# Summing K·q over the head dimension: one more halving on VectorE for most of K, and one shared PSUM bank and read for its first half

## The chip, the cores and the metric

One core of one Trainium2 chip runs the kernel. The metric is the device time of one execution in microseconds (us). Each experiment was timed in rounds together with the kernel before on the same chip.

## The reference

```python
# q: [8, 32, 1, 128], k and v: [8, 32, 4096, 128], all bf16
scores = einsum('bhqd,bhkd->bhqk', q, k) * 128 ** -0.5
attn = softmax(scores, axis=-1)
return einsum('bhqk,bhkd->bhqd', attn, v)
```

There is one query per head, 256 heads, and 537 MB of K and V that are each used once.

## The kernel before

A tile is 8 heads of K (or V): 128 partitions (16 to a head) by 256 keys by 128 numbers, 64 KB in each partition, 8.39 MB in all. There are 32 K tiles and 32 V tiles. Three buffers hold them in rotation, in the order K(t+1), V(t), K(t+2), V(t+1) and so on. By this order V(t) takes over the buffer of K(t), and K(t+1) that of an older V.

```python
kv_pool = ctx.enter_context(tc.tile_pool(name="kv_pool", bufs=SLOTS))   # SLOTS = 3

def product(t, lo, hi):                 # VectorE, in place in the K tile
    part = kt[:, lo:hi, :]
    tensor_tensor(out=part, in0=part, in1=q, op=mult)
    tensor_tensor(out=part[:, :, 0:64], in0=part[:, :, 0:64], in1=part[:, :, 64:128], op=add)
    if width_of(t, lo // UC) < D // 2:  # second half of K, tiles 1 to 28
        tensor_tensor(out=part[:, :, 0:32], in0=part[:, :, 0:32], in1=part[:, :, 32:64], op=add)

def sum_over_d(t, u):                   # TensorE: identity matmuls add column groups in PSUM
    n = width_of(t, u) // DS            # DS = 8 columns of 64 keys fill a bank
    for s in range(n):
        matmul(ps, lhsT=ident, rhs=kt[:, u*UC:(u+1)*UC, s*DS:(s+1)*DS], start=(s == 0), stop=(s == n-1))

def scores_of(t, u):                    # VectorE: the last 8 columns, out of PSUM
    tensor_reduce(out=sc[:, u*UC:(u+1)*UC], in_=ps, op=add)

# ... one tile in the steady part (cuts; Q = 64 keys):
product(t, 0, 2*Q);   sum_over_d(t, 0); sum_over_d(t, 1)
product(t, 2*Q, 3*Q); sum_over_d(t, 2); scores_of(t, 0); scores_of(t, 1)
product(t, 3*Q, C);   sum_over_d(t, 3); scores_of(t, 2)
values_loop(t - 1)                      # TensorE, 64 matmuls over V(t-1)
load("k", t + 1)                        # waits for values_loop(t - 2), which ran in the turn of tile t - 1
load("v", t)                            # waits for sum_over_d(t, 3), the last reader of K(t)
scores_of(t, 3); weights_of(t)
```

## Time and profile before

| | kernel before |
|---|---|
| time, median of the runs beside the changed kernel | 1251.66 us |
| load queue, share of 16 engines' span | 99.5% |
| VectorE / TensorE busy | 1021.9 us (82%) / 786.8 us (63%) |
| K landing to K landing, mean of tiles 2 to 29 | 38.86 us |
| V issue after K's landing, mean | 32.16 us |

"Landing" of a K here is the start of the first product on it, which waits for that load. The prediction shows the page's lines and one steady tile and says how to read them. One line of the view of waits adds who waited, for what, total us, times, longest.

```profile
DVE kt L191 <- DMA kt<-in_k_dram: 139.9, 28, 6.3
```

VectorE waits for K 28 times, 5.0 us each: it is ahead of the loads by that much.

### The profile page before, as it was taken

The page shows a single profiled execution, that of the slowest core. Times are in us where ns is not written, and L with a number is a line of the kernel's source. Part 1 is how long each engine was busy: PE and PEld are TensorE (multiplying, and loading weights), DVE is VectorE, ACT ScalarE, POOL GpSimd, SP SyncE. Part 2 cuts the span into 40 slices and gives each one's busy share as a digit, 9 for nine tenths or more (in the row PEclk, how much of TensorE's full clock was granted, in tenths as well). Part 3 has the DMA queues.
Part 4 walks back from the last instruction along what each step waited for, and adds up shares of the span by engine and source line. Part 5 has one row for each costly group of instructions (what it writes and reads, how often), then busy time and mean ns, then how long its engine had stood idle before and what let it go on. Part 6 is the DMA issues. An engine that isn't in the chain of part 4 may idle for free. (4 is left out here: it accounts for less than half of the span.)

```text
span 1250.2 us, 10842 instructions
## 1 busy us (share of the span) xinstructions
PE 786.8 (63%) x3116; PEld 299.6 (24%) x3116; DVE 1021.9 (82%) x495; ACT 166.1 (13%) x433; POOL 4.5 (0%) x24
## 2 busy tenths in 40 slices
PE   3366567666576655766558665577655776556755
PEld 1122123222232222322223222222222222212222
DVE  7887987878977789777798777987779877798783
ACT  0111011111011110111101111011110111101111
POOL 1000000000000000000000000000000000000000
PEclk9987788777888778877788777887778878779867
DMA  9999999999999999999999999999999999999997
GB/s 405 436 436 435 434 436 432 436 430 428 426 437 436 429 435 434 434 435 436 436 434 432 424 437 437 432 430 428 436 437 434 430 433 434 430 435 421 427 446 329
DMA packets 11432, 537.33 MB, mean 430 GB/s; under 512 B 1808, under 2 KB 2064, under 8 KB 2320
## 3 DMA queue, kind: packets, MB, share of 16 engines
q1 hardware_dynamic: 11072, 536.94, 99.5%
q8 instruction: 15, 0.25, 0.1%
q10 hardware_dynamic: 336, 0.07, 0.0%
q14 instruction: 9, 0.07, 0.0%
HBM read 536.94 MB, written 0.07 MB: 430 GB/s over the span
## 5 line engine op out<-in xcount | busy, mean ns | idle before, releaser
L191 DVE TENSOR_TENSOR kt<-kt,qb 128x8192 bf16<-128x8192 bf16 (+1 forms) x99 | 560.9, 5665 | 146.6 <-DMA kt<-in_k_dram 139.9
L211 PE MATMUL ps<-kt,ident 128*128 128x512 bf16 x800 | 278.4, 511 | 389.9 <-DVE kt L199 299.7
L294 PE MATMUL av<-vt,w 128*32 x1740 | 425.5, 397 | 4.6
L194 DVE TENSOR_TENSOR kt<-kt 128x4096 bf16<-128x4096 bf16 (+1 forms) x99 | 288.8, 2917 | 3.4
L294 PEld LDWEIGHTS av<-vt,w 128*32 x1740 | 173.4, 100 | 262.4 <-issue 119.5
L211 PEld LDWEIGHTS <-ident 128*128 128x128 bf16 x800 | 95.7, 120 | 565.4 <-issue 527.9
L223 DVE TENSOR_REDUCE sc<-ps 128x64 f32<-128x512 f32 x128 | 85.3, 685 | 54.0 <-PE ps L211 54.0
L248 ACT ACTIVATE e<-sc,nmax 128x256 bf16<-128x256 f32 x32 | 16.3, 508 | 706.7 <-DVE nmax L242 706.7
L255 ACT ACTIVATE w<-e,mine 128x256 bf16<-128x256 bf16 x256 | 105.6, 495 | 1.1
L199 DVE TENSOR_TENSOR kt<-kt 128x2048 bf16<-128x2048 bf16 x56 | 68.6, 1225 | 1.9
L351 ACT ACTIVATE comb<-av 32x512 bf16<-32x512 f32 (+1 forms) x32 | 18.8, 586 | 329.0 <-PEq L284 321.4
L280 PE MATMUL av<-vt,w 128*32 128x512 bf16 x116 | 47.2, 499 | 14.6 <-issue 13.1
L371 PE MATMUL op<-comb,pick 32*16 32x128 bf16 (+1 forms) x128 | 12.1, 213 | 20.7 <-ACT comb L351 20.7
L280 PEld LDWEIGHTS av<-vt,w 128*32 128x32 bf16 x116 | 6.9, 100 | 55.2 <-issue 55.2
L177 PE MATMUL qp<-qg,heads 8*128 8x128 bf16 x32 | 7.0, 217 | 16.7 <-ACT qg L175 16.7
L371 PEld LDWEIGHTS <-pick 32*16 32x16 bf16 (+1 forms) x128 | 8.7, 83 | 27.7 <-issue 27.3
L322 PE MATMUL av<-vt,w 128*32 128x512 bf16 x188 | 13.7, 418 | 2.3 <-DMA vt<-in_v_dram 2.3
L235 DVE TENSOR_REDUCE pmax<-sc 128x1 f32<-128x256 f32 x32 | 13.4, 420 | 1.1
L175 ACT ACTIVATE qg<-qh 8x128 bf16<-8x128 f32 x32 | 8.5, 266 | 33.5 <-PE qh L171 33.5
L171 PE MATMUL qh<-q_all,ident 128*8 128x128 bf16 x32 | 7.2, 225 | 8.7 <-DMA q_all<-in_q_dram 8.3
L179 ACT ACTIVATE qb<-qp 128x128 bf16<-128x128 f32 x32 | 8.9, 278 | 9.7 <-PE qp L177 9.7
L237 DVE TENSOR_SCALAR spread<-same,pmax 128x32 f32<-128x32 f32 x32 | 7.7, 242 | 1.1
(31 smaller groups left out, 47.7 us busy)
## 6 DMA issues: line engine op xcount, KB each, us to landing
kt<-in_k_dram SPq DMA_DIRECT2D x4, 4096.0 KB, 24.3
kt<-in_k_dram SPq DMA_DIRECT2D x4, 2048.0 KB, 13.0
vt<-in_v_dram SPq DMA_DIRECT2D x1, 4096.0 KB, 33.9
vt<-in_v_dram SPq DMA_DIRECT2D x1, 2048.0 KB, 38.5
vt<-in_v_dram SPq DMA_DIRECT2D x1, 1024.0 KB, 40.5
vt<-in_v_dram SPq DMA_DIRECT2D x1, 512.0 KB, 41.3
vt<-in_v_dram SPq DMA_DIRECT2D x31, 25.8
kt<-in_k_dram SPq DMA_DIRECT2D x29, 28.3
```

Of the source, the lines that this page charges most:

```text
L191: nc.vector.tensor_tensor(out=part, in0=part, in1=qb[:].to_broadcast([P, hi - lo, D]), op=ALU.mult)
L194: nc.vector.tensor_tensor(out=part[:, :, 0 : D // 2], in0=part[:, :, 0 : D // 2], in1=part[:, :, D // 2 : D], op=ALU.add,)
L199: nc.vector.tensor_tensor(out=part[:, :, 0 : D // 4], in0=part[:, :, 0 : D // 4], in1=part[:, :, D // 4 : D // 2], op=ALU.add,)
L211: nc.tensor.matmul(ps[:], lhsT=ident[:], rhs=kt[:, u * UC : (u + 1) * UC, s * DS : (s + 1) * DS], start=(s == 0), stop=(s == n - 1),)
L223: made = nc.vector.tensor_reduce(out=scs[t][:, u * UC : (u + 1) * UC], in_=sums.pop((t, u))[:], axis=AX.X, op=ALU.add)
L248: nc.scalar.activation(out=e[:], in_=sc[:], func=ACT.Exp, bias=nmax[:, 0:1], scale=scale, accum_out=esums[t // R][:, t % R : t % R + 1],)
L255: nc.scalar.activation(out=w[:, :, g, :], in_=e_g, func=ACT.Copy, scale=mine[:, 0, g : g + 1])
L280: pe.matmul(av, lhsT=wf[:, i * nw : (i + 1) * nw], rhs=vf[:, i * nv : (i + 1) * nv], **how)
L294: pe.matmul(av, lhsT=wf[:, bass.ds(ow + i * nw, nw)], rhs=vf[:, bass.ds(ov + i * nv, nv)], start=False, stop=False,)
L322: nc.tensor.matmul(avs[t][j * AG : (j + 1) * AG, :], lhsT=w[:, i, :, :], rhs=vt[:, c0 : c0 + CB, :], start=(i < TG), stop=(j not in group[ ...
L351: nc.scalar.activation(out=comb[0:n, :, :], in_=av[0:n, :, :], func=ACT.Copy)
L371: nc.tensor.matmul(ops[n][:], lhsT=pick[0:e, m, r, :], rhs=comb[0:e, m, :], start=(r == 0 and m == 0), stop=(r == R - 1 and m == CB - 1 an ...
```

## The change

The change moves work from TensorE to VectorE: each further halving of the 128 columns is one more add in place, and leaves half as many columns for the identity matmuls. With 16 columns left, the whole first half (128 keys by 4 columns) fits one bank, so four matmuls and one read do for it. Tile 0 and the last three keep their widths. The diff, cut:

```diff
-        return D // 4 if u >= NU // 2 and 0 < t < NT - 3 else D // 2
+        return (D // 4 if lo == C // 2 else D // 8) if 0 < t < NT - 3 else D // 2
 ... in product
+        n = D
+        while n > width_of(t, lo):
+            n //= 2
             nc.vector.tensor_tensor(
+                out=part[:, :, 0:n], in0=part[:, :, 0:n], in1=part[:, :, n : 2 * n], op=ALU.add
             )
 ... in sum_over_d
-        n = width_of(t, u) // DS
+        ds = BANK // (hi - lo)
+        n = width_of(t, lo) // ds
 ... in the tile loop (cut)
-                sum_over_d(t, 0)
+                sum_over_d(t, 0, HALF)
-                scores_of(t, 0)
-            scores_of(t, 1)
+                scores_of(t, 0, HALF)
```

More of the change, by code (lines that the diff above doesn't have):

```diff
@@ L43 @@
     scale = float(D) ** -0.5
-    UC = 64
-    DS = 512 // UC
-    NU = C // UC
+    BANK = 512
     CB = 4
@@ L180, in q_prep, with width_of @@
         qbs[t] = qb
-    def width_of(t, u):
-        return D // 4 if u >= NU // 2 and 0 < t < NT - 3 else D // 2
+    def width_of(t, lo):
+        return (D // 4 if lo == C // 2 else D // 8) if 0 < t < NT - 3 else D // 2
     def product(t, lo, hi):
@@ L193, in product, with sum_over_d, scores_of @@
         )
-        nc.vector.tensor_tensor(
-            out=part[:, :, 0 : D // 2], in0=part[:, :, 0 : D // 2],
-            in1=part[:, :, D // 2 : D], op=ALU.add,
-        )
-        if width_of(t, lo // UC) < D // 2:
+        n = D
+        while n > width_of(t, lo):
+            n //= 2
             nc.vector.tensor_tensor(
-                out=part[:, :, 0 : D // 4], in0=part[:, :, 0 : D // 4],
-                in1=part[:, :, D // 4 : D // 2], op=ALU.add,
+                out=part[:, :, 0:n], in0=part[:, :, 0:n], in1=part[:, :, n : 2 * n], op=ALU.add
             )
     sums = {}
-    def sum_over_d(t, u):
+    def sum_over_d(t, lo, hi):
         kt = loads["k", t]
-        ps = ps_s.tile([P, UC, DS], F32, name="ps", tag="ps")
-        n = width_of(t, u) // DS
+        ps = ps_s.tile([P, BANK], F32, name="ps", tag="ps")
+        ds = BANK // (hi - lo)
+        n = width_of(t, lo) // ds
         for s in range(n):
             nc.tensor.matmul(
-                ps[:], lhsT=ident[:],
-                rhs=kt[:, u * UC : (u + 1) * UC, s * DS : (s + 1) * DS],
+                ps[:], lhsT=ident[:], rhs=kt[:, lo:hi, s * ds : (s + 1) * ds],
                 start=(s == 0), stop=(s == n - 1),
             )
-        sums[t, u] = ps
+        sums[t, lo] = ps
     scs = {}
-    def scores_of(t, u):
-        if u == 0:
+    def scores_of(t, lo, hi):
+        if lo == 0:
             scs[t] = sc_pool.tile([P, C], F32, name="sc", tag="sc")
+        ps = sums.pop((t, lo))[:].rearrange("p (c s) -> p c s", c=hi - lo)
         made = nc.vector.tensor_reduce(
-            out=scs[t][:, u * UC : (u + 1) * UC], in_=sums.pop((t, u))[:], axis=AX.X, op=ALU.add
+            out=scs[t][:, lo:hi], in_=ps, axis=AX.X, op=ALU.add
         )
-        if u == NU - 1:
+        if hi == C:
             behind_loop(made)
@@ L392, in store_of @@
             nc.scalar.dma_start(o_n[s, :, lo : u + 1, :], stages[s][:, lo : u + 1, :])
-    Q = C // 4
+    Q, HALF = C // 4, C // 2
     load("k", 0)
@@ L408 @@
                 load("v", t)
-            product(t, 0, 2 * Q if loop else Q)
-            if not loop:
-                sum_over_d(t, 0)
+            if loop:
+                product(t, 0, HALF)
+            else:
+                product(t, 0, Q)
+                sum_over_d(t, 0, Q)
             if 0 < t - 1 <= LT:
@@ L419 @@
             if loop:
-                sum_over_d(t, 0)
+                sum_over_d(t, 0, HALF)
             else:
-                product(t, Q, 2 * Q)
-            sum_over_d(t, 1)
-            if not loop:
-                scores_of(t, 0)
-            product(t, 2 * Q, 3 * Q)
-            sum_over_d(t, 2)
+                product(t, Q, HALF)
+                sum_over_d(t, Q, HALF)
+                scores_of(t, 0, Q)
+            product(t, HALF, HALF + Q)
+            sum_over_d(t, HALF, HALF + Q)
             if loop:
-                scores_of(t, 0)
-            scores_of(t, 1)
+                scores_of(t, 0, HALF)
+            else:
+                scores_of(t, Q, HALF)
             if t > 2 and t % R == 1:
                 recip_of(n)
-            product(t, 3 * Q, C)
-            sum_over_d(t, 3)
-            scores_of(t, 2)
+            product(t, HALF + Q, C)
+            sum_over_d(t, HALF + Q, C)
+            scores_of(t, HALF, HALF + Q)
             if loop:
@@ L441 @@
                 values_of(t - 1, 0, C)
-            scores_of(t, 3)
+            scores_of(t, HALF + Q, C)
             weights_of(t)
```

## The prediction

> **What bounds the kernel now.** I read the page from the top: busy shares, the forty slices, the DMA queues, then the DMA issues.
>
> ```profile
> PE 786.8 (63%) x3116; PEld 299.6 (24%) x3116; DVE 1021.9 (82%) x495; ACT 166.1 (13%) x433; POOL 4.5 (0%) x24
> ...
> DMA  9999999999999999999999999999999999999997
> GB/s 405 436 436 435 434 436 432 436 430 428 426 437 436 429 435 434 434 435 436 436 434 432 424 437 437 432 430 428 436 437 434 430 433 434 430 435 421 427 446 329
> ...
> q1 hardware_dynamic: 11072, 536.94, 99.5%
> ...
> HBM read 536.94 MB, written 0.07 MB: 430 GB/s over the span
> ...
> vt<-in_v_dram SPq DMA_DIRECT2D x31, 25.8
> kt<-in_k_dram SPq DMA_DIRECT2D x29, 28.3
> ```
>
> Every slice but the last has the DMA engines at 90% or more, and the load queue fills 99.5% of 16 engines' span. VectorE is the busiest engine and has 18% of the span to spare. K and V have to be read once: 2 x 8 x 32 x 4096 x 128 x 2 bytes = 536.9 MB, which is what was read. The end is therefore set by the loads. The 64 KB packets of the trace take 2.42 us each, so 16 engines move 16 x 65536 / 2.42 = 433 GB/s, and 536.9 MB at that rate are 1239 us. The other 11 us of the 1250.2 us span are the launch before the first byte, the short packets at both ends and the work after the last V rows. The change touches none of these: the first tile and the last three keep two-fold halving and 64-column sums exactly as they are.
>
> The question is then only whether the changed compute still lets every load be issued before the queue runs dry. Three buffers hold K and V tiles of 8.39 MB. V of tile t goes into the buffer of K of tile t, so its issue waits for the last identity matmul that reads that K tile; the next K goes into the buffer of an older V, so its issue waits for the loop of value matmuls. I follow one steady iteration in the timeline (columns: start us, us, engine, line, operation, tiles, count, idle time before).
>
> ```profile
> 618.41 0.33 SPq L158 DMA_DIRECT2D vt<-in_v_dram  x1
> ...
> 619.63 14.81 PE L294 MATMUL av<-vt,w 128*32 x60
> ...
> 624.96 8.69 DVE L191 TENSOR_TENSOR kt<-kt,qb 128x16384 bf16<-128x16384 bf16 x1 [4.88 <-DMA kt<-in_k_dram]
> ...
> 633.69 4.42 DVE L194 TENSOR_TENSOR kt<-kt 128x8192 bf16<-128x8192 bf16 x1
> ...
> 635.26 0.33 SPq L158 DMA_DIRECT2D kt<-in_k_dram  x1
> ...
> 642.49 2.29 DVE L194 TENSOR_TENSOR kt<-kt 128x4096 bf16<-128x4096 bf16 x1
> 644.81 1.23 DVE L199 TENSOR_TENSOR kt<-kt 128x2048 bf16<-128x2048 bf16 x1
> 645.96 1.28 DVE L223 TENSOR_REDUCE sc<-ps 128x64 f32<-128x512 f32 x2
> ...
> 655.21 1.87 PE L211 MATMUL ps<-kt,ident 128*128 128x512 bf16 x4 [7.80 <-DVE kt L199]
> ...
> 657.11 0.33 SPq L158 DMA_DIRECT2D vt<-in_v_dram  x1
> ...
> 663.67 8.69 DVE L191 TENSOR_TENSOR kt<-kt,qb 128x16384 bf16<-128x16384 bf16 x1 [4.89 <-DMA kt<-in_k_dram]
> ```
>
> From K landing to K landing are 663.67 - 624.96 = 38.71 us, two tiles at 433 GB/s. VectorE has finished its tile and sits idle 4.9 us until the next K lands. V is issued 32.15 us after the K landing, 6.5 us before the queue needs it. The same lead comes out of the issue table: a V takes 25.8 us from issue to landing, of which a tile's transfer is 19.35 (half of 38.71), so it stood 6.4 us in the queue; a K stood 28.3 - 19.35 = 9.0 us. These two leads are the slack that the change spends.
>
> **What the Trainium skill says.** "VectorE: DVE Perf Modes", section "The perf-mode tier table": a bf16 tensor_tensor in SBUF reaches the 2x mode, 1224 ns for 2048 elements; a tensor_reduce has only 1x. The trace agrees: 1225 ns for the 128x2048 add, and 685 ns for a reduce of 512 fp32. "TensorE: Matmul & The Clock Gate", Part 1: after about 3.4 us of idling the array runs at half clock, 426.7 ns between matmuls of 512 columns against 215.7 warm. The trace agrees: the four matmuls ahead of each V issue, after 7.8 us of idling, take 1.87 us, whereas sixteen in a row at 638.17 take 3.61. "SBUF — State Buffer", section "Who interferes with whom": DMA and compute engines use separate SBUF ports, so a busier VectorE should not slow the loads. This trace neither contradicts nor isolates it: slices with VectorE at 7 and at 9 tenths both show 436 GB/s. "DMA: Bandwidth & Descriptors", Specifications, puts the fabric ceiling at 435 GB/s; the 433 of the packets is already there.
>
> **The change part by part**, for each of the 28 tiles 1 to 28.
> - Added on VectorE, first half: an add of 128x4096 (2.29 us) and one of 128x2048 (1.22). From start to start, which includes the handoffs, such adds cost 4.46, 2.32 and 1.15 (651.61 to 653.93 to 655.08 in the timeline for the last two). The half takes 8.73 + 4.46 + 2.32 + 1.15 = 16.66 us against 638.03 - 624.96 = 13.07: +3.59.
> - Removed: one of the two PSUM reads after the third quarter. Two took 1.19 start to next start, so one takes 0.60: -0.59. The new read still streams 512 elements and only writes 128 sums, so I keep 685 ns.
> - Added, last quarter: an add of 128x1024. The rows of 8192, 4096 and 2048 elements (4425, 2292, 1225 ns) lie on a line of 0.521 ns an element plus 158, giving 692 ns; with a handoff +0.73. The 8192 and 4096 rows differ in the number of runs, and the 2048 row has shorter runs, yet one line fits all three, so I charge nothing for runs of 16 elements.
> - Removed on TensorE: the first half needs 16 columns / 4 = 4 matmuls instead of 2 x 8, the last quarter 2 instead of 4: 14 fewer per tile, 392 in all, so 408 stay of 800. On the path to the V issue lie only the last quarter's: 1.87 us becomes about 1.87 - 2 x 0.427 = 1.02: -0.85.
>
> Sum on the path from K landing to V issue: 3.59 - 0.59 + 0.73 - 0.85 = **+2.9 us**. V's lead falls from 6.5 to about 3.6 us. The value loop starts right after those sums, as before, and starts cold as before, so I keep 16.85 us from V issue to K issue; K's lead falls from 9.0 to about 6.1 us. VectorE's idle time before each K tile falls from 4.9 to about 2.0 us. Busy time: VectorE + 28 x (2.29 + 1.22 + 0.69 - 0.69) = +98 us, to about 1120 us (90%). TensorE loses 392 matmuls; at 0.427 to 0.511 each (cold spacing and recorded mean) this is 170 to 200 us of 787, none of which the end waits for.
>
> None of the leads goes to zero, so no load starts later and **the sum at the end is 0**: predicted 1251.5 us, the time before. The tightest place is the start, where V of tile 1 is issued at 74.82 while K of tile 2 lands at 80.95. Its lead of about 6 us loses the same 2.9, so it is not lost either.
>
> **The rivals.** (a) VectorE becomes the bound. For it: at 90% the share looks near the limit, and the work per tile goes to about 36.7 us from first product to last statistic (33.8 now, 624.96 to 658.78, plus 2.9). Against: the loads give it 38.71. It would need another 2 us a tile; if adds over runs of 16 elements fell to the 1x rate, an estimate from 0.521 doubled is 2048 x 0.521 + 1024 x 0.521 = 1.6 us. That only just fits; if everything exceeded the period by 1 us, the kernel would be 28 us slower, about 1280. (b) The issue comes too late although VectorE has room: the lead of 3.6 us could be shorter than what a load needs between its issue and its first bytes. First evidence: the first K is issued at 0.81 us and bytes flow from about 1.9, so 1.1 us is enough. If each V left a bubble of 0.3 us, 28 x 0.3 = 8 us, 1260. (c) TensorE, with less work, stays cold longer and the value loop lengthens: entirely cold, 60 matmuls are 25.6 us instead of 14.8, K's lead of 6.1 would become -4.7, and 28 x 4.7 = 130 us would be added, 1380. Against it: the loop already begins cold after 8 us of idling in the profile and gets its full clock within 4 us, and the change leaves the loop itself alone. (d) A gain: fewer matmuls and more granted clock. All of it lands in idle time of TensorE; even with no DMA idling at all the 0.5% that the queue leaves free are 6 us, 1245.
>
> **Range and chances.** The three runs of before lie within 0.3 us, and I expect the loads to set the same pace, so the range is narrow: 1249.8 to 1255.0. The upper side allows a few small bubbles of (b) or a slow add of (a). A gain over 2% (25 us) would need the loads to run above the rate they hold now: 1%. A loss over 2% needs (a) or (c) in full: 3%. Within 2%: 96%.
>
> **What would show it.** Right: DMA slices as before; VectorE near 1120 us; 100 PSUM reads; 408 sum matmuls; idle time before the products on K landing falling from 139.9 to about 60 us; V from issue to landing near 22.9 us and K near 25.4; the chain of waits still ending in the V loads. Wrong: adds of 128x2048 with runs of 16 well above 1.22 us, V landing 20 us or less after its issue, DMA slices at 8 tenths, products no longer waiting for K loads, or a value loop over 20 us. A period above 38.8 us between K landings would make the prediction wrong.

## The result, and the profile after

The changed kernel takes **1267.32 us** (1265.66 to 1268.20, four runs) against 1251.66 us: ratio 1.0123, interval 1.0108 to 1.0138. It is within 2%, as forecast, but 15.7 us slower and far outside the predicted range of 1249.8 to 1255.0.

The page of the changed kernel (busy shares, DMA slices, load queue, rate over the span, chain that ended last, issue to landing):

```profile
PE 688.0 (54%) x2724; PEld 252.0 (20%) x2724; DVE 1122.4 (89%) x550; ACT 166.0 (13%) x433; POOL 4.4 (0%) x24
...
DMA  9999999999999999999999999999999999999998
...
q1 hardware_dynamic: 11072, 536.94, 99.2%
...
HBM read 536.94 MB, written 0.07 MB: 424 GB/s over the span
...
DMA vt<-in_v_dram 3%; DVE kt L189 1%; PE ps L207 0%; PE av L318 0%; DVE kt L195 0%; SPq L156 0%; DVE sc L219 0%; PE op L359 0%; ACT stage L378 0%; PE op L367 0%; DVEq L219 0%
...
vt<-in_v_dram SPq DMA_DIRECT2D x31, 24.2
kt<-in_k_dram SPq DMA_DIRECT2D x29, 26.7
```

The DMA slices look exactly as full as before, yet the same bytes come at 424 GB/s, not 430. A share of 99% does not say that the engines move bytes at their full rate: it counts the time that packets are under way. One steady tile of the timeline shows the compute side:

```profile
634.05 8.69 DVE L189 TENSOR_TENSOR kt<-kt,qb 128x16384 bf16<-128x16384 bf16 x1 [2.17 <-DMA kt<-in_k_dram]
...
642.77 8.01 DVE L195 TENSOR_TENSOR kt<-kt 128x8192 bf16<-128x8192 bf16 x3
...
647.21 0.33 SPq L156 DMA_DIRECT2D kt<-in_k_dram  x1
...
658.62 0.69 DVE L219 TENSOR_REDUCE sc<-ps 128x128 f32<-128x512 f32 x1
...
663.67 4.28 DVE L195 TENSOR_TENSOR kt<-kt 128x4096 bf16<-128x4096 bf16 x3
...
668.01 1.03 PE L207 MATMUL ps<-kt,ident 128*128 128x512 bf16 x2 [7.36 <-DVE kt L195]
...
669.07 0.33 SPq L156 DMA_DIRECT2D vt<-in_v_dram  x1
...
673.43 8.69 DVE L189 TENSOR_TENSOR kt<-kt,qb 128x16384 bf16<-128x16384 bf16 x1 [2.68 <-DMA kt<-in_k_dram]
```

The adds, the read and the two last matmuls cost what was worked out, and V is issued 669.07 - 634.05 = 35.02 us after K's landing. By form, the adds have these means (28 of the 84 work on runs of 16 elements, the others on 32; all 28 of the second line on 16):

```profile
L195 DVE TENSOR_TENSOR kt<-kt 128x2048 bf16<-128x2048 bf16 x84 | 102.9, 1225 | 2.9
L195 DVE TENSOR_TENSOR kt<-kt 128x1024 bf16<-128x1024 bf16 x28 | 19.4, 691 | 1.0
```

VectorE is still not the bound: it waits for K in every tile. In the view of waits:

```profile
DVE kt L189 <- DMA kt<-in_k_dram: 74.6, 28, 4.1
```

That is 2.7 us a tile, more than the 2.0 predicted, because the landings themselves now come later: 39.38 us apart here, 39.43 in the mean. Over the 27 intervals from tile 2 to tile 29, 39.43 - 38.86 makes 15.6 us: the whole loss.

So the loads are slower although the queue never shows as empty. The trace also has each 64 KB packet with start and duration (7680 of them). I joined packets to engines by their times (the record does not name the engine, so such chains can swap where two engines' times coincide). Start and duration, both in us, of a few engines around the V issue at 669.07 in the changed kernel:

```
663.55:2.42 665.96:2.42 668.38:2.43 670.80:3.15 673.95:2.42 676.37:2.42
663.48:2.42 665.90:2.44 668.33:2.45 670.78:3.14 673.92:2.42 676.33:2.42
664.54:2.43 666.96:2.42 669.38:2.42 671.80:2.68 674.48:2.42 676.90:2.42
662.86:2.42 665.27:2.42 667.69:2.50 670.18:2.70 672.89:2.42 675.30:2.42
```

In each engine shown, the packet that starts 1 to 3 us after the issue takes 2.7 to 3.2 us, where nearly all others take 2.42 (the longest of the run near an issue takes 4.1). In the last row this packet still belongs to K: the stretch does not spare the engines that are behind. In the changed kernel 534 packets last over 2.5 us, before only 52. Most of them start from 1 to 5 us after a V issue; there is no such crowd after K issues. Summed over the packets from one V issue to the following K issue and divided by 16 engines, the time over 2.42 us plus the time in which engines carried no packet is 0.65 us a tile against 0.03 before; 27 tiles of the difference are 16.7 us. That is about the loss again, from the other side.

**Theory A** follows: V is issued too late. Not later than the landing of K, but later than the moment at which the engines have taken their last K packet and want the first of V. A tile is 128 packets, so in order of start the first packet of V can be counted off. It starts 2.9 us before "K has landed" in the kernel before. Little of that is the wait from the last packet's end to the product: the last K packet of the tile shown ends at 672.97, 0.46 us ahead of 673.43. The rest is that the 16 engines are not in step. The trace has sixteen finish signals for each load, each some 0.3 us after a packet's end; those of this K come from 671.04 to 673.31, so the first engine needs V's packets while the last still carries K. In the kernel before, the signals of one K lie 1.7 us apart at tile 3 and 4.2 us apart at tile 26. So V's lead in the kernel before was not 6.5 us but 3.7 in the mean, and it falls along the run from 5.9 to 2.3 as the engines drift apart. In the changed kernel it is 1.6 in the mean, and never below 0.96: an engine then waits for the issue. (Reckoned from the first of K's finish signals, less 0.3 us, the two means are 3.7 and 1.5.) The **rival B** is that more VectorE work in SBUF slows the transfers themselves.

### The profile page after: what moved, and what is told of

Its sections match the earlier page's. It is cut to its first block, busy times and chain, and to the rows that moved or that the text cites. A ratio compares the mean times of both kernels' runs of the same rounds, so it can differ in the third digit from the quotient of the medians.

```text
span 1265.7 us, 10145 instructions
## 1 busy us (share of the span) xinstructions
PE 688.0 (54%) x2724; PEld 252.0 (20%) x2724; DVE 1122.4 (89%) x550; ACT 166.0 (13%) x433; POOL 4.4 (0%) x24
## 5 line engine op out<-in xcount | busy, mean ns | idle before, releaser
L195 DVE TENSOR_TENSOR kt<-kt 128x8192 bf16<-128x8192 bf16 (+2 forms) x239 | 475.2, 1988 | 8.2
L207 PE MATMUL ps<-kt,ident 128*128 128x512 bf16 x408 | 174.9, 578 | 508.5 <-DVE kt L195 508.2
L290 PE MATMUL av<-vt,w 128*32 x1740 | 429.9, 408 | 1.2
L290 PEld LDWEIGHTS av<-vt,w 128*32 x1740 | 178.9, 103 | 258.2 <-issue 101.2
L207 PEld LDWEIGHTS <-ident 128*128 128x128 bf16 x408 | 41.6, 122 | 634.8 <-DVE kt L195 571.1
L219 DVE TENSOR_REDUCE sc<-ps 128x64 f32<-128x512 f32 (+1 forms) x99 | 68.0, 687 | 31.0 <-PE ps L207 31.0
L175 PE MATMUL qp<-qg,heads 8*128 8x128 bf16 x32 | 7.0, 217 | 16.7 <-ACT qg L173 16.7
```

Of the source, the lines that this page charges most:

```text
L195: nc.vector.tensor_tensor(out=part[:, :, 0:n], in0=part[:, :, 0:n], in1=part[:, :, n : 2 * n], op=ALU.add)
L207: nc.tensor.matmul(ps[:], lhsT=ident[:], rhs=kt[:, lo:hi, s * ds : (s + 1) * ds], start=(s == 0), stop=(s == n - 1),)
L219: made = nc.vector.tensor_reduce(out=scs[t][:, lo:hi], in_=ps, axis=AX.X, op=ALU.add)
L290: pe.matmul(av, lhsT=wf[:, bass.ds(ow + i * nw, nw)], rhs=vf[:, bass.ds(ov + i * nv, nv)], start=False, stop=False,)
```

## The experiments

In each, "V at" is the mean delay from K's landing to V's issue, and "slow" counts the 64 KB packets over 2.5 us.

**1. The kernel before, V issued later, VectorE untouched.** Matmuls whose result is thrown away come ahead of the last sum:

```diff
+        for s in range(LATE if u == NU - 1 and 0 < t < NT - 3 else 0):   # LATE = 7
+            nc.tensor.matmul(ps[:], lhsT=ident[:], rhs=kt[:, u*UC:(u+1)*UC, 0:DS], start=True, stop=True)
         for s in range(n):
```

> The kernel before, with seven more identity matmuls (results thrown away) ahead of the last sum of each tile 1 to 28. VectorE's work is untouched; only the issue of V moves from 32.15 us after the landing of K to about 35, as in the changed kernel. Theory A (the V load is issued too late: its first packets run slow because its lead was shorter than I worked out): 1262 to 1272 us, and several hundred 64 KB packets over 2.5 us as in the changed kernel (534), not 52. Rival B (more VectorE work in SBUF slows the transfers themselves): 1251.5 us within 1, packets as before.

Measured: 1266.22 us against 1251.92 (ratio 1.0113, interval 1.0096 to 1.0130), V at 34.86 us, 444 slow packets. VectorE stays at its old load:

```profile
PE 822.6 (65%) x3312; PEld 308.1 (24%) x3312; DVE 1021.9 (81%) x495; ACT 166.1 (13%) x433; POOL 4.4 (0%) x24
```

The loss comes back without any of the change's VectorE work. A is right in kind and in size. K's issue moves with V's here, as in the changed kernel, because the value loop starts after the last sums. But counted in the same way, K's lead in the changed kernel is still 5.1 us in the mean (6.7 before) and never below 3.95, and only 4 of its 534 slow packets start 1 to 5 us after a K issue. So the late issue that costs is V's.

**2. The kernel before, VectorE busier, V issued as before.** Fifteen small adds on zeros after the statistics:

```diff
             weights_of(t)
+            if loop:
+                for _ in range(15):
+                    nc.vector.tensor_tensor(out=w_last[:, 0:LAST//2, :], in0=w_last[:, 0:LAST//2, :],
+                                            in1=w_last[:, LAST//2:LAST, :], op=ALU.add)
```

> The kernel before, with fifteen small adds on zeros (about 3.4 us a tile) on VectorE after the statistics of each tile 1 to 28, when it waits for the next K. VectorE busy rises to about 1115 to 1120 us as in the changed kernel; V is issued as before. Theory A (late issue): 1251.5 us within 1. Rival B (VectorE work slows the transfers): about 1267 us.

Measured: 1255.72 us, ratio 1.0029 (1.0013 to 1.0046), VectorE 1116.5 us, V at 32.17, 124 slow packets. Neither theory expected this: far from B's 1267, but 3.8 us over the time beside it, where A expected none. Experiments 5 and 6 look into it.

**3. The changed kernel, V issued 0.6 us earlier.** The read of the first half moves behind the last quarter's product:

```diff
-            if loop:
-                scores_of(t, 0, HALF)
-            else:
+            if not loop:
                 scores_of(t, Q, HALF)
 ...
             sum_over_d(t, HALF + Q, C)
+            if loop:
+                scores_of(t, 0, HALF)
             scores_of(t, HALF, HALF + Q)
```

> The changed kernel, with the PSUM read of the first half moved from before the last quarter's product to after it. The work is the same in sum, but the last sums and with them the issue of V come 0.6 us earlier (34.4 us after the landing of K, not 35.0). Theory A: most of the loss depends steeply on the lead, so part of it goes: 1256 to 1264 us. Rival B: 1267 us within 1.5.

Measured: 1259.02 us (ratio 1.0061, 1.0044 to 1.0078), V at 34.45, 228 slow packets. The same work in another order, 0.6 us earlier, saves over half of the loss: A.

**4. The changed kernel with half buffers.** Six buffers of half a tile, and two loads of 4 MB for each tile, so the first half of V waits only for the first half of K:

```diff
-    kv_pool = ...tile_pool(name="kv_pool", bufs=SLOTS)
+    kv_pool = ...tile_pool(name="kv_pool", bufs=2 * SLOTS)
-        buf = kv_pool.tile([P, C, D], ...)
-        for n in cuts.get((kind, t), [C]):
+        for n in cuts.get((kind, t), [H, H]):          # H = C // 2
+            h, x = divmod(c0, H)
+            if x == 0: buf[h] = kv_pool.tile([P, H, D], ...)
 ... (the value loop is cut in two, one for each half of V)
```

> The changed kernel, with each K and V tile in two half buffers and two loads of 4 MB: the first half of V needs only the first half of K to be done, so it is issued more than 15 us earlier. VectorE's work is the same 1122 us. Theory A: the loss is gone, 1249.5 to 1252.5 us, few packets over 2.5 us. Rival B: 1265 us or more.

Measured: 1257.41 us (ratio 1.0044, 1.0028 to 1.0061). The first half of V is issued at 18.39 us. Both expectations miss: 9.9 us of the loss are gone, 5.5 us stay. The packets are now 32 KB, and only 24 of 16000 last over 1.26 us, so none crowd after an issue. But they take 1.2176 us in the mean, where half a 64 KB packet of the kernel before takes 1.2119. That is 16000 x 0.0057 / 16 = 5.7 us. Experiment 12 is the control.

**5. The extra VectorE work as one instruction.**

```diff
             weights_of(t)
+            if loop:
+                spare = small.tile([P, 1], F32, name="spare", tag="spare")
+                nc.vector.tensor_reduce(out=spare[:],
+                    in_=loads["v", t - 1][:, 0:26, :].rearrange("p c d -> p (c d)"), axis=AX.X, op=ALU.add)
```

> The kernel before, with the extra VectorE work as one long reduce of 3328 elements of the V tile (about 3.6 us) in the idle time after the statistics, in place of the fifteen small adds that cost 3.8 us in the run before. Theory A (the fifteen adds cost through their number: more instruction fetches on the DMA engines, which push engines apart and eat the lead of V): 1251.9 us within 1. Rival B (VectorE traffic in SBUF while K lands and V starts slows the transfers): 1255 us or more.

Measured: 1252.81 us (ratio 1.0009, 0.9993 to 1.0026), 29 slow packets. VectorE is as busy as in experiment 2, and the time is that of before within the interval. So VectorE's busy time as such costs nothing that shows, and something else in experiment 2 does, the number of instructions being the likeliest. Of B this run tests little: it reads 3328 elements a tile, where the change adds three adds of 4096, 2048 and 1024 with two inputs and an output each. Against B stand experiments 1, 4 and 12.

**6. The fifteen adds, V issued 0.6 us earlier.** The kernel of experiment 2, with `scores_of(t, 1)` moved behind `sum_over_d(t, 3)`.

> The kernel with the fifteen small adds, and one PSUM read moved behind the last quarter's product, so V is issued 0.6 us earlier (31.55 us after the landing of K). VectorE's work is unchanged. Theory A: the earlier issue gives back most of the 3.8 us, 1251.5 to 1253.5 us. Rival B: 1255.5 us within 1.

Measured: 1255.50 us (ratio 1.0033, 1.0016 to 1.0049), V at 31.56, 78 slow packets. **A's expectation fails here**: slow packets go from 124 to 78 and the time does not move. The rows of instruction fetches in the DMA view (queue, packets, MB, share), first before, then the fifteen adds:

```profile
q8 instruction: 15, 0.25, 0.1%
q10 hardware_dynamic: 336, 0.07, 0.0%
q14 instruction: 9, 0.07, 0.0%
```

```profile
q8 instruction: 15, 0.25, 0.1%
q10 hardware_dynamic: 336, 0.07, 0.0%
q14 instruction: 13, 0.11, 0.0%
```

The 8 KB fetches of the last row run on the engines that carry the loads. One takes 0.31 us, and in several cases the load packet behind it takes up to 0.7 us more: that engine is then 1.0 us late. If it is the last engine to finish, the whole tile is. In the run with fifteen adds the landings are 38.7 us apart, but 39.63 to 39.67 at four tiles spaced four apart, each with such a fetch inside; in the kernel before only two intervals have this length (39.66 and 39.64). Not every fetch lengthens its tile. From tile 1 to tile 29 the landings take 2.9 us more in all than before, and moving the issue cannot help against an engine that is late by itself. Part of it is a short lead all the same: with the engines further out of step, V's lead is 3.05 us in the mean, though V's delay is unchanged, and 64 slow packets start 1 to 5 us after a V issue against 15 before. Experiment 6 brings the lead to 3.42 and these packets to 53 only. This rests on the traces and on experiment 5; I made no run that changes the fetches alone, so what the fifteen adds cost is argued and not shown.

**7. Four extra matmuls** in place of seven (`LATE = 4`).

> The kernel before with four extra matmuls ahead of the last sum, so that V is issued some 1.7 us later (about 33.8 us after the landing of K, between the kernel before and the changed one). Theory A: 1254 to 1260 us. Rival B: 1251.9 us within 1.

Measured: 1254.40 us (ratio 1.0018, 1.0001 to 1.0035), V at 33.80, 178 slow packets.

**8. Twelve extra matmuls** (`LATE = 12`).

> The kernel before with twelve extra matmuls, so that V is issued 36 to 37 us after the landing of K, later than in the changed kernel (35.05). Theory A: with no lead left the period is the issue's delay plus a fixed 4.4 us (39.43 - 35.05 in the changed kernel), 40.4 to 41.4 us, and the time 1290 to 1320 us. Rival B: 1251.9 us within 1.

Measured: 1273.78 us (ratio 1.0170, 1.0151 to 1.0190), V at 35.96, 559 slow packets. The loss grows, but less than I expected: the interval between landings is 39.74 us, 3.8 us over V's delay and not 4.4. The engines' lead differs from tile to tile, and the intervals scatter from 38.7 to 41.6, so a mean delay plus a constant is too crude.

**9. The first half's part of the change alone**: the last quarter is halved twice as before.

```diff
-        return (D // 4 if lo == C // 2 else D // 8) if 0 < t < NT - 3 else D // 2
+        return (D // 4 if lo >= C // 2 else D // 8) if 0 < t < NT - 3 else D // 2
```

> The part of the change in the first half alone: halved three times, one bank, one read; the last quarter is halved twice as before. By the sums of the prediction V is issued at 32.15 + 3.59 - 0.59 = 35.15 us after the landing of K, as in the changed kernel (35.05), though VectorE works 19 us less. Theory A: 1265 to 1269 us, as the changed kernel. A theory that goes by VectorE's share would give back about a fifth of the loss, 1264.

Measured: 1270.07 us (ratio 1.0145, 1.0128 to 1.0162), V at 35.18, 497 slow packets, and VectorE does 19 us less than in the changed kernel:

```profile
PE 711.9 (56%) x2780; PEld 254.2 (20%) x2780; DVE 1103.0 (87%) x522; ACT 166.1 (13%) x433; POOL 4.4 (0%) x24
```

Less VectorE work, and 1 us above A's range instead of below: the first half's adds carry the whole loss, and the last quarter's third halving gives a little back, as its sum of +0.73 - 0.85 says.

**10. The last quarter's part alone**, on the kernel before.

```diff
-        return D // 4 if u >= NU // 2 and 0 < t < NT - 3 else D // 2
+        return (D // 8 if u == NU - 1 else D // 4) if u >= NU // 2 and 0 < t < NT - 3 else D // 2
 ... (product adds the third halving where the width is D // 8)
```

> The part in the last quarter alone, on the kernel before: its third halving costs VectorE 0.73 us a tile and saves two cold matmuls, 0.85 us, ahead of the issue of V, so V is issued at about 32.0 us. Theory A: 1251.5 us within 1. By VectorE's share: 1254.

Measured: 1252.47 us (ratio 1.0007, 0.9990 to 1.0024), V at 32.04, 30 slow packets: no difference that this run can tell from none.

**11. The kernel before, V issued 0.6 us earlier** (`scores_of(t, 1)` moved as in experiment 6).

> The kernel before with one PSUM read moved behind the last quarter's product: V is issued 0.6 us earlier, at 31.55 us. Theory A: its loads hardly wait any more for V's issue, so little is to be had, 1250.8 to 1251.6 us.

Measured: 1251.57 us (ratio 1.0002, 0.9985 to 1.0019), V at 31.57, 22 slow packets. More lead than the kernel before has is worth nothing, so no order of this work will beat it by much.

**12. The kernel before with half buffers**, edited as in experiment 4.

> The kernel before with half buffers and 4 MB loads, the control for the changed kernel with half buffers (1257.4 us). If the 5.5 us left there come from the rows of 32 KB in place of 64 KB (16000 packets of 1.2176 us against half as many of 2.4218 are 6.6 us more on 16 engines), this kernel takes 1257 us too, within 1. If they come from VectorE's work, it takes 1251.6.

Measured: 1257.08 us (ratio 1.0044, 1.0027 to 1.0061). It is as slow as the changed kernel with half buffers, 1257.41. With V's issue out of the way, the two kernels are 0.3 us apart (their medians are from different rounds), though the changed one's VectorE is busy 1122.2 us and this one's 1021.9. The 5.5 us belong to the half buffers, and the longer packets account for them: with the mean of all 7680 packets, 2.4239 us (the expectation says 2.4218), its sum is 5.7 us.

Put in order of V's issue, kernels with quite different VectorE loads form one row:

| kernel | VectorE busy, us | V at, us | slow packets | time, us |
|---|---|---|---|---|
| before, read later (11) | 1021.9 | 31.57 | 22 | 1251.57 |
| last quarter alone (10) | 1041.2 | 32.04 | 30 | 1252.47 |
| before | 1021.9 | 32.16 | 52 | 1251.66 |
| four extra matmuls (7) | 1021.9 | 33.80 | 178 | 1254.40 |
| changed, read later (3) | 1120.4 | 34.45 | 228 | 1259.02 |
| seven extra matmuls (1) | 1021.9 | 34.86 | 444 | 1266.22 |
| changed | 1122.4 | 35.05 | 534 | 1267.32 |
| first half alone (9) | 1103.0 | 35.18 | 497 | 1270.07 |
| twelve extra matmuls (8) | 1021.8 | 35.96 | 559 | 1273.78 |

The knee lies between 32.16 and 33.80 us. No kernel tried beats the kernel before.

The traces allow a sharper sorting: by V's lead at every single issue, over these nine kernels and those of experiments 2, 5 and 6 (V of tiles 2 to 27, 312 issues). Packet time over 2.42 us from 2 us before V's issue to K's issue, and engine time without a packet from V's issue to K's, divided by 16 engines, make the loss at an issue:

| V's lead, us | mean loss, us: six kernels with VectorE at 1041 us or less | six kernels with VectorE at 1103 us or more |
|---|---|---|
| under 1 | 1.17 (25 issues) | 1.18 (12) |
| 1 to 2 | 0.43 (18) | 0.56 (48) |
| 2 to 3 | 0.14 (49) | 0.16 (50) |
| over 3 | 0.02 (64) | 0.02 (46) |

The loss goes with the lead, and a busy VectorE changes it little if at all: the largest difference, 0.13 us, is within the scatter of those issues.

## Why the prediction was wrong

- **The bound was read correctly.** The loads set the end before and after, and the chain of waits still ends in them.
- **The sums of the change were right.** V's issue was to move by +2.9 us; it moved from 32.16 to 35.05. VectorE was to reach 1120 us and reached 1122.4. There were 408 sum matmuls as foretold. The adds cost 1225 and 691 ns, with no charge for runs of 16 elements. Reads were 99, not 100: tile 29 also shares its bank, contrary to my statement that the last three tiles keep everything as it was.
- **The step that failed**: "V is issued 32.15 us after the K landing, 6.5 us before the queue needs it", and with it "a V takes 25.8 us from issue to landing, of which a tile's transfer is 19.35, so it stood 6.4 us in the queue". Both measure the need from the landing of K, which is the moment at which the last of 16 engines has finished; and from its first packet to its landing a V takes not 19.35 but 22.4 us. The first engine wants V's packets 2.9 us sooner in the mean. The lead was 3.7 us, and what was left of it after the change was not 3.6 but 0.8 on paper; the loads then slipped until it was 1.6.
- **A second step failed with it**: rival (b), that the issue comes too late though VectorE has room, was the right one, and I set it aside with "1.1 us is enough", read from the launch. The floor of 0.96 us agrees with that figure, but packets that start 1 to 3 us after an issue run slow as well. (b) was sized at 0.3 us a tile; it measured 0.58. The sign that the prediction named for being wrong came true: the period rose above 38.8 us, to 39.43.
- **The other rivals.** (a) VectorE as the bound: no, it waits 2.7 us for each K. (c) A longer value loop: no; from V's issue to K's the mean is 16.9 us after and before. TensorE's granted clock fell from 0.81 to 0.73, and that left this time as it was.
- V of tile 1 was named the tightest place. In fact leads shrink along the run, and the early tiles have the most. In the kernel before the lead falls from 3.78 to 2.80 us after tile 18 and from 2.91 to 2.25 after tile 25; these are the two intervals of 39.66 and 39.64 us, and each has a fetch inside.
- One reading was wrong without harm: "slices with VectorE at 7 and at 9 tenths both show 436 GB/s". The seven slices at 9 tenths show 426 to 435. That VectorE is not what slows the loads is shown by experiments 1, 4 and 12, not by the slices.

What stays open is how a late issue stretches the packets of that moment, rather than only delaying them.

The skill's page "DMA: Bandwidth & Descriptors", section "Anatomy of one DMA — SWDGE (gpsimd) path", says that most of the fixed 2 us of a DMA lies after its last byte, in the confirmation of the write. It speaks of another issuing path, and this case does not show such a time: the finish signals come some 0.3 us after the packets' ends, so the 2.9 us are mostly the engines' drift.

## What to carry to other kernels

How early a load is issued must be measured against the time at which the first engine runs out of the packets before it, not against the landing of the load before, which is the last engine's: here the two are 2.9 us apart. A queue that shows 99% busy can still lose time in stretched packets, so look at packet durations just after each issue. In these kernels a lead of over 3 us to the load's first packet cost next to nothing (0.02 us an issue), and one under 1 us cost 1.2 us an issue, even though the engine that grew has time to spare. Counted to the landing of the load before, a lead of 4.9 us already cost 2.8 us in all (V at 33.80 us of 38.7, a loss just clear of its interval). Whether other load sizes need the same lead, no run here shows.

## What the Trainium skill lacked or had wrong

- "DMA: Bandwidth & Descriptors" gives about 600 ns for HWDGE's first byte (section "Latency and other measured facts"), but not how long ahead an issue must be to keep a running queue at its rate. Here the first packets start no sooner than 0.96 us after the issue begins (0.33 us of it the issue itself), and packets starting within some 3 us take up to 4.1 us in place of 2.42. Leads over 3 us cost 0.02 us an issue, leads under 1 us 1.2.
- No page that I read says how far the 16 engines of one queue drift apart: the sixteen finish signals of one K were 1.7 us apart at tile 3 and 4.2 at tile 26 of the kernel before, and V's lead fell from 5.9 to 2.3 us. An 8 KB instruction fetch, with the slower packet behind it, made one engine up to 1.0 us late.
- The same DMA page advises large transfers by their total size. At 4 MB against 8 MB, with rows of 32 KB in place of 64 KB, a packet still took 0.5% longer a byte, and the kernel 1257.08 us against 1251.61; no run separates the row length from the load size.
- "SBUF — State Buffer" says in "Who interferes with whom" that engines do not slow DMA. The runs agree: with half buffers, the changed kernel's 100 us more of VectorE work left the ratio to the kernel before at 1.0044, as without it.
